# Moving more additions of a long convolution from VectorE to DMA, beside attention

## The chip, the cores and the metric

The kernel runs on one core of a Trainium2 chip. The metric is the time of one execution on the device in microseconds (us), the median of several runs. TensorE is called PE here, VectorE DVE, ScalarE ACT, GpSimd POOL and SyncE SP, as in the profile.

## The reference

Two independent halves are computed and set side by side. One is a state-space convolution over 576 channels: a kernel of 2048 taps is made for each channel from 128 complex modes, and applied as a causal convolution (the reference does it with a Fourier transform of twice the length). The other is attention with 32 query heads of width 18 that share one key and one value head. All is in float32.

```python
dt = exp(log_dt)[:, None];  A = A_re + 1j*A_im                      # [576, 128]
P = exp((dt*A)[:, :, None] * arange(2048))                           # [576, 128, 2048]
K = einsum("dn,dnl,dn->dl", C, P, dt*B).real                         # the taps
y = irfft(rfft(pad(u.T)) * rfft(pad(K)))[:, :2048].T + u * Dskip     # half A, [2048, 576]

q = (x @ wq) as 32 heads of 18;  k = x @ wk;  v = x @ wv             # x: [2048, 576]
p = softmax(q k^T * 18**-0.5);   o = p v                             # per head
out = concatenate([y, o @ wo], -1)                                   # [2048, 1152]
```

## The kernel before

**One planned order.** PE, ACT and DVE take their instructions in an order that the program itself writes out while it is built (`manual_schedule`); POOL and SP are ordered by the scheduler of the language. A small model of the clocks, `Clock` (`t` for PE, `v` for DVE, `a` for ACT), says when each engine would be free. The parts of the work are generators, wrapped in `Stream`. They yield what they need next: `"v"` with a time (go on once the clock is there), `"p"` (PE work, when there is room), `"w"` (ask again at the next step), `"b"` (a block of ACT work). On the chip nothing is timed by this model: it sets the order alone, and semaphores make each engine wait for its operands.

**Attention** (`Attention.main`) goes over 4 chunks of 512 queries, 8 groups of 4 heads, 16 blocks of 128 keys. For each of 1024 pairs of heads and key block, `scores` (L493) puts two matmuls into PSUM, `exponentials` (L504) is one ACT instruction of 128 x 1024, and `product` (L802) multiplies by the values. Three score buffers are in flight. Between the groups of three pairs, `fill` lets the other streams place work on PE: the projection of the next queries (`qproj`, `queries`), the output projection (`outproj`) and the convolution. Queries go to DRAM (`qd`, `sd`, on POOL's queue) and come back in another layout (`aug`, on SP's).

**The convolution** (`Conv`) goes over 12 chunks of 48 channels. Its `front(k)` makes the taps:

- `factors` (with `arguments`): exponentials, sines and cosines of 26 positions for each channel and mode; the modes lie on the partitions. For two chunks at a time ACT does them, and those of the odd chunk are put into DRAM (`park`) and loaded back. In `r` and `f` (real and imaginary part, `[P, 48, 26]`) the positions are innermost. `sm` is `r + f`, `df` is `f - r` for the last ten positions.
- `tables(k, s)`, twice a chunk (`NSB = 2`, 24 channels each): each power is the product of two factors. For each of three groups of columns DVE does three products and two additions (the five rows of `tab` and `tt`).
- `kgen` (L1168): small matmuls of one part of the table with the other, 48 a bank, evacuated by DVE into `ksb`. The taps go through DRAM (`kd`) into `kt` with the partitions rearranged.

`back(k)` convolves. `transform` turns `u` and the taps into spectra `us` and `ks` with matmuls and DVE additions, and the sums of real and imaginary parts that the three-product form needs are added by DMA (L1240 for `us`, L1253 for `ks`). The time axis is four blocks, so the product of the spectra is a convolution over blocks: for each half of the rows (`h`), four products `pt` of shrinking size are added to `acc` by DVE. Then one DMA adds within `acc` (L1275), DVE combines, and the inverse transform `iy` adds onto `u * Dskip`, which is stored to `outa`.

**Front and back** are joined by `turn`: the streams are `back(k)` and `front(k + 1)`, and the next two begin when both have ended.

```python
        if self.n < NCK and not any(st.live for st in self.streams):
            self.n += 1
            k = self.n
            self.streams = [Stream(self.back(k, self.kt), self.k)] if k < NCK else []
            if k + 1 < NCK:
                self.streams.append(Stream(self.front(k + 1), self.k))
```

L128 and L132 are helper lines of `Vector`, through which nearly all of DVE's additions, products and copies go, and L202 one for matmuls; there the tiles' names tell the groups apart.

Of the kernel before, what the change touches and what calls it, by code (L numbers as in the profile page):

```python
# [17 lines left out]
P = 128  # L18
# [22 lines left out]
RATE = 3.6754  # L41
PACE = 2.761
AHEAD = 0.3494
TOTAL = 577.1437
LAST = 608.4461
DEFER = 0.378
NAUG = 5
LEFT = 2.1255
CAP = 1.4306
DEBT = 0.6525  # L50
GROUP = 0.1637
HOLD = 0.1219
LEAD = 1.5045
MOST = 0.4717
LEAST = 0.4946
NEAR = 0.9404
SLOPE = 0.7408
SOON = 1.1606
URGENT = 11.0338
BACK = 2  # L60
HELD = 0
GAP = 0.2773
GAP_NEW = 0.3388
# [5 lines left out]
NSB = 2  # L69
# [3 lines left out]
MAGIC = 12582912.0  # L73
TWO_PI = 6.283185
# [130 lines left out]
class Attention:  # L205
# [36 lines left out]
    def setup(self, tp, conv):  # L242
# [19 lines left out]
        self.ident = cp.tile([P, P], F32, name="ident")  # L262
# [159 lines left out]
    def queries(self, c, m, qh, ql, aw):  # L422
# [41 lines left out]
        sh = self.p2.tile([8, CT], F32R, tag="sh", name=f"sh{c}_{m}", bufs=1)  # L464
        V.tensor_scalar(sh, un[0:8, 0:1].broadcast_to([8, CT]), -1.0, None, op0=ALU.mult)
# [5 lines left out]
        q.dma_start(sd[h0 + n0:h1, :], sh[:h1 - h0 - n0, :].bitcast(F32))  # L471
# [495 lines left out]
class Conv:  # L967
# [57 lines left out]
    def arguments(self, k, w, f, r, m):  # L1025
# [11 lines left out]
        shp = [P, ND, NF]  # L1037
        ch = lambda t: t.unsqueeze(2).broadcast_to(shp)
        row = lambda j: self.pos[:, j, :].unsqueeze(1).broadcast_to(shp)
# [21 lines left out]
    def factors(self, k):  # L1061
# [4 lines left out]
        shp = [P, ND, NF]  # L1066
        ch = lambda t, n: t.unsqueeze(2).broadcast_to([P, ND, n])
# [4 lines left out]
        if k % 2:  # L1072
            n = ND * NF
            for j, t in enumerate((f, r, m, w)):
                nc.sync.dma_start(t, self.parked[:, j * n:min((j + 1) * n, 3 * n + 3 * ND)].rearrange("p (c n) -> p c n", n=t.shape[2]))
            yield "v", K.t + 7.0, False
        else:
            two = p1.tile([P, 3 * ND * NF + 3 * ND], F32, tag="tab", name=f"two{k}")
            part = lambda j, n: two[:, j * ND * NF:j * ND * NF + n * ND].rearrange("p (c n) -> p c n", n=NF if n == NF else ND)
# [26 lines left out]
        c8 = lambda t: t[:, :, 0:8]  # L1106
        t1 = p1.tile([P, ND, 8], F32, tag="tmp", name=f"t1_{k}")
        t2 = p1.tile([P, ND, 8], F32, tag="dif", name=f"t2_{k}")
        tt(t2, c8(r), ch(w[:, 1, :], 8), op=mu)
        tt(t1, c8(f), ch(w[:, 1, :], 8), op=mu)  # L1110
        yield "v", 0.0, False
        tt(c8(r), c8(r), ch(w[:, 0, :], 8), op=mu)
        tt(c8(f), c8(f), ch(w[:, 0, :], 8), op=mu)
# [3 lines left out]
        sm = p1.tile(shp, F32, tag="sum", name=f"sum{k}")  # L1117
        df = p1.tile([P, ND, 10], F32, tag="dif", name=f"dif{k}")
        yield "v", 0.0, False
        tt(df, f[:, :, 16:], r[:, :, 16:], op=sb)  # L1120
        yield "v", 0.0, False
        tt(sm, r, f, op=ad)
# [3 lines left out]
    def tables(self, k, s):  # L1126

        nc, V, p1 = self.nc, self.V, self.pf
        tt = V.tensor_tensor
        n = ND // NSB  # L1130
        r, f, sm, df = (t[:, s * n:(s + 1) * n, :] for t in self.fac)
        tab = p1.tile([P, 2, n, 96], F32, tag="tab", name=f"tab{k}_{s}")
        for j, t in enumerate((r, f)):
            V.tensor_copy(tab[:, j, :, 0:8], t[:, :, 0:8])
            V.tensor_copy(tab[:, j, :, 32:40], t[:, :, 8:16])

        for lo, hi, dst, j0, j1 in ((0, 16, 8, 0, 3), (8, 19, 40, 0, 4), (8, 19, 40, 4, 7)):
            nj = j1 - j0
            shp = [P, n, nj, 8]
            L = lambda t: t[:, :, lo:lo + 8].unsqueeze(2).broadcast_to(shp)  # L1140
            H = lambda t, o=0: t[:, :, hi - o + j0:hi - o + j1].unsqueeze(3).broadcast_to(shp)
            re, im = (tab[:, j, :, dst + 8 * j0:dst + 8 * j1].rearrange("p c (j l) -> p c j l", l=8) for j in range(2))
            t = p1.tile(shp, F32, tag="tmp", name=f"tt{k}_{s}_{lo}_{j0}")
# [3 lines left out]
            yield "v", 0.0, False  # L1147
            tt(t, L(f), H(sm), op=ALU.mult)
            yield "v", 0.0, False
            tt(im, im, re, op=ALU.add)  # L1150
            yield "v", 0.0, False
            tt(re, re, t, op=ALU.subtract)
            if (lo, j0) != (8, 4):
                yield "v", 0.0, False
        self.tab = tab

    def kgen(self, k, s, ksb):
        nc, K = self.nc, self.k
        tab = K.v + 0.3
        for q in range(2):  # L1160
            yield "p", max(tab, K.fill), False
            ps = self.bank(TB // 2 * 64, f"kg{k}_{s}_{q}").rearrange("p (d c) -> p d c", c=64)
            ds = slice(q * TB // 2, (q + 1) * TB // 2)
            for d in range(TB // 2):
                for j in range(2):
                    for g in range(4):
                        t = self.tab[:, j, g * TB + ds.start + d, :]
                        nc.tensor.matmul(ps[32 * g:32 * g + 32, d, :], t[:, :32], t[:, 32:],  # L1168
                                         start=(j == 0), stop=(j == 1), tile_position=(0, 32 * g))
            K.pe(0.665)  # L1170
            self.evacuate()
            self.V.tensor_copy(ksb[:, :, s, :, ds], ps.rearrange("p d (h c) -> p h c d", h=4))
            self.evacuated()

    def front(self, k):

        nc = self.nc
        yield from self.factors(k)
        ksb = self.pf.tile([P, 4, NSB, 16, TB], F32, tag="ksb", name=f"ksb{k}")
        for s in range(NSB):  # L1180
            yield from self.tables(k, s)
            yield from self.kgen(k, s, ksb)
# [48 lines left out]
    def back(self, k, kt):  # L1231
# [7 lines left out]
        nc.sync.dma_start(us[:, 0:4, :], us[:, 4:8, :])  # L1239
        nc.gpsimd.dma_start(us[:, 0:4, :], us[:, 8:12, :], accum_op=ALU.add)  # L1240
        ks = p1.tile([P, 12, NE], F32, tag="ks", name=f"ks{k}")
        yield from self.transform(lambda r: kt[:, :, :, 4 * r:4 * r + 4, :].rearrange("p g s b d -> p (g s) (b d)"), ks[:, 4:12, :], f"k{k}", self.kt_ready)
        self.kt = None
        k2, kd, ka = ks[:, 0:4, :], ks[:, 4:8, :], ks[:, 8:12, :]
        v = lambda t, b0, b1: t.rearrange("p q (c n) -> p (q c) n", n=4 * TB)[:, :, b0 * TB:b1 * TB]
# [5 lines left out]
        tt(kd, ka, k2, op=ALU.subtract)  # L1251
        yield "v", 0.0, False
        nc.gpsimd.dma_start(ka, k2, accum_op=ALU.add)  # L1253
        done = K.v + 8.0
        blk = lambda t, b0, b1: t.rearrange("p q (c b d) -> p (q c) b d", b=4, d=TB)[:, :, b0:b1, :]
        acc = p1.tile([P, 12, NE], F32, tag="acc", name=f"acc{k}")
        n = 6 * NE // TB // 4
        for h in range(2):
            if h == 1:
                yield "v", done, False  # L1260
            for m in range(4):
                shp = [P, n, 4 - m, TB]
                at = lambda t, b0, b1: blk(t, b0, b1)[:, h * n:(h + 1) * n]
                kb = at(ks, m, m + 1).broadcast_to(shp)
                if m == 0:
                    tt(at(acc, 0, 4), at(us, 0, 4), kb, op=ALU.mult)
                    yield "v", 0.0, False
                else:
                    t = p1.tile(shp, F32, tag="sc", name=f"pt{k}_{m}_{h}")
                    tt(t, at(us, 0, 4 - m), kb, op=ALU.mult)  # L1270
                    yield "v", 0.0, False
                    tt(at(acc, m, 4), at(acc, m, 4), t, op=ALU.add)
                    yield "v", 0.0, False
# [213 lines left out]
```

## Time and profile before

| | |
|---|---|
| three runs | 1188.77, 1191.43, 1191.72 us (median 1191.43) |
| the profiled execution | 1191.61 us, of which the span of its instructions is 1189.8 us |
| mean granted PE clock | 0.991 of full speed |
| bytes moved by DMA | 132.22 MB, mean 111 GB/s |

How to read it: a row of a group gives line, engine, operation, output and input tiles, shapes and count, then the busy time in us and the mean of one in ns, then how long the engine was idle just before these instructions and what ended that. The chain is the work that ended last, followed back from the last instruction; its shares say by which engine the time passed. A row of the timeline gives start, duration, engine, line and operation, and in brackets the idle time before it with what ended it. `x` is a count.

### The profile page before, as it was taken

To read this page: it belongs to the slowest core of one execution; us is meant where nothing else is said; L and a number is where in the kernel's file an instruction comes from. 1 tells how busy PE (TensorE), PEld (TensorE's weight loads), DVE (VectorE), ACT (ScalarE), POOL (GpSimd) and SP (SyncE) were. 2 spreads that over 40 slices of the span, in tenths; PEclk is the share of its full clock that TensorE was granted. 3 is DMA by queue.
4 is the path that set the end of the run, shared out by engine and by line. 5 is a ranking of instruction groups with operands and counts; after the bars stand their busy time and mean duration, and the time that the engine had idled before them with its cause. 6 is when DMAs were issued, how large, how long until landed. Compare 5 with 4: busy or idle time off the path is not lost.

```text
span 1189.8 us, 41346 instructions
## 1 busy us (share of the span) xinstructions
PE 1136.8 (96%) x17954; PEld 604.1 (51%) x17954; DVE 960.9 (81%) x1698; ACT 1039.8 (87%) x1095; POOL 86.9 (7%) x140
## 2 busy tenths in 40 slices
PE   7999999998999989999989999999999999999997
PEld 2455555554555545555545555544544545555553
DVE  6858969885996996697799699699699797699485
ACT  5999889987888988988898888998999998899993
POOL 1100200101010100011020000001000000000000
PEclk9999999999999999999989999999999999999999
DMA  8542444425232331424353421234422431431222
GB/s 297 169 143 74 137 140 100 151 80 183 65 121 81 103 128 66 154 64 115 110 172 103 152 73 50 98 98 130 140 72 66 131 122 58 156 88 39 90 56 70
DMA packets 57097, 132.22 MB, mean 111 GB/s; under 512 B 7732, under 2 KB 18068, under 8 KB 55631
## 3 DMA queue, kind: packets, MB, share of 16 engines
q1 hardware_dynamic: 45647, 100.60, 24.4%
q0 software_dynamic: 10544, 28.19, 10.0%
q8 instruction: 143, 2.34, 0.8%
q10 hardware_dynamic: 720, 0.73, 0.2%
q14 instruction: 43, 0.35, 0.1%
HBM read 61.51 MB, written 48.45 MB: 92 GB/s over the span
## 4 chain that ended last, share of the span: by engine, by line
PE 64%; DVE 23%; ACT 5%; DMA 4%; issue 3%; SPq 0%; ACTq 0%; DVEq 0%
PE ops L802 26%; PE s L493 18%; DVE tab L128 6%; DVE acc L128 3%; PE op L202 3%; PE q L202 3%; ACT P L504 3%; PE iy L202 3%; PE kg L1168 3%; DVE ks L128 2%; DVE pt L128 2%; PE lk L202 1%; PE hk L202 1%; PE lu L202 1%; DVE tt L128 1%
## 5 line engine op out<-in xcount | busy, mean ns | idle before, releaser
L504 ACT ACTIVATE P<-s 128x1024 f32<-128x1024 f32 x992 | 941.6, 1031 | 114.3 <-PE s L493 105.6
L802 PE MATMUL ops<-P,v_sb 128*32 128x256 f32 x8192 | 536.1, 383 | 4.4 <-DVE o L132 2.8
L493 PE MATMUL s<-aug,kaug 55*128 55x512 f32 x2048 | 350.8, 439 | 7.1 <-ACT P L504 6.0
L802 PEld LDWEIGHTS ops<-P,v_sb 128*32 128x32 f32 x8192 | 247.2, 110 | 185.8 <-issue 52.2
L493 PEld LDWEIGHTS s<-aug,kaug 55*128 55x128 f32 x2048 | 167.9, 185 | 201.9 <-ACT P L504 107.9
L202 PE MATMUL op<-wo_sb,oT 126*32 126x288 f32 (+1 forms) x1152 | 84.3, 410 | 8.2 <-DVE ob L132 7.6
L202 PE MATMUL q<-x,wq_sb 128*32 128x256 f32 x1200 | 79.3, 390 | 4.5 <-DVE ql L128 2.4
L132 DVE COPY ksb<-kg 128x192 f32<-128x192 f32 x48 | 17.6, 367 | 66.3 <-PE kg L1168 66.1
L128 DVE TENSOR_TENSOR tab<-tab,tt 128x576 f32<-128x576 f32 (+1 forms) x72 | 59.1, 820 | 1.3
L128 DVE TENSOR_TENSOR tab<-sum,r 128x576 f32<-128x576 f32 (+1 forms) x72 | 58.7, 816 | 0.0
L128 DVE TENSOR_TENSOR tt<-f,sum 128x576 f32<-128x576 f32 (+1 forms) x72 | 58.7, 815 | 0.0
L128 DVE TENSOR_TENSOR tab<-tab 128x576 f32<-128x576 f32 (+1 forms) x72 | 58.7, 815 | 0.0
L128 DVE TENSOR_TENSOR tab<-r,dif 128x576 f32<-128x576 f32 (+1 forms) x72 | 58.7, 815 | 0.0
L128 DVE TENSOR_TENSOR acc<-acc,pt 128x864 f32<-128x864 f32 (+2 forms) x72 | 54.4, 755 | 1.7
L202 PEld LDWEIGHTS op<-wo_sb,oT 126*32 126x32 f32 (+1 forms) x1152 | 32.4, 109 | 45.1 <-DVE ob L132 13.1
L202 PEld LDWEIGHTS q<-x,wq_sb 128*32 128x32 f32 x1200 | 36.2, 111 | 36.7 <-issue 11.3
L128 DVE TENSOR_TENSOR pt<-us,ks 128x864 f32<-128x864 f32 (+2 forms) x72 | 54.0, 750 | 0.6
L1240 POOL DMA_DIRECT2D us<-us x12 | 11.8, 980 | 517.0 <-PE lk L202 84.6
L1168 PEld LDWEIGHTS kg<-tab 128*32 128x32 f32 x2304 | 36.7, 110 | 13.9 <-issue 5.9
L128 DVE TENSOR_TENSOR scu<-lu,scu 128x384 f32<-128x384 f32 x48 | 24.5, 551 | 23.6 <-PE lu L202 23.5
L1168 PE MATMUL kg<-tab 128*32 128x64 f32 x2304 | 41.8, 220 | 1.5 <-DVE tab L128 0.9
L128 DVE TENSOR_TENSOR u<-u,iy 128x384 f32<-128x384 f32 x24 | 13.3, 554 | 32.8 <-PE iy L202 32.8
(162 smaller groups left out, 1039.5 us busy)
## 6 DMA issues: line engine op xcount, KB each, us to landing
aug<-qd SPq DMA_DIRECT2D x124, 108.0 KB
park<-two SPq DMA_DIRECT2D x6, 1944.0 KB
od<-o SPq DMA_DIRECT2D x31, 256.0 KB
qd<-qh POOLq DMA_DIRECT2D x30, 256.0 KB, 3.5
u<-u SPq DMA_DIRECT2D x12, 480.0 KB
kd<-ksb SPq DMA_DIRECT2D x12, 384.0 KB
kt<-kd SPq DMA_DIRECT2D x48, 96.0 KB
us<-us SPq DMA_DIRECT2D x12, 384.0 KB
```

The lines of the kernel that those rows point to most:

```text
L128: return self.v.tensor_tensor(out, a, b, **k)
L132: return self.v.tensor_copy(out, src)
L202: nc.tensor.matmul(ps[j:e], w[:, j:e], x, start=start, stop=stop, tile_position=(0, j))
L493: nc.tensor.matmul(ps[:, j, :], self.kaug[r, kb * P:(kb + 1) * P], t[r, :], start=True, stop=True)
L504: nc.scalar.activation(pt, ps, AF.Exp, scale=SCALE)
L802: nc.tensor.matmul(o_ps[32 * j:32 * j + 32, cs], self.v[:, kb, :], pts[2 * n + j // 2][:, j % 2, cs], start=(kb + f == 0), stop=(kb + f == ...
L1168: nc.tensor.matmul(ps[32 * g:32 * g + 32, d, :], t[:, :32], t[:, 32:], start=(j == 0), stop=(j == 1), tile_position=(0, 32 * g))
L1240: nc.gpsimd.dma_start(us[:, 0:4, :], us[:, 8:12, :], accum_op=ALU.add)
```

## The change

- **Tables.** Four sub-blocks of 12 channels instead of two of 24. DVE does three products a group and no addition: two are written into the table, and the third, `t`, is added by one DMA on POOL's queue to real and imaginary part alike (`t` is read twice). Two table buffers alternate, and `kgen` of a sub-block comes after the products of the next. The groups have 3, 3 and 4 rows of eight columns. Three `t` buffers.
- **Order of dimensions.** In `r`, `f`, `sm`, `df` and the tables the channels are innermost. A column of the table that `kgen` hands to PE has its words 12 apart. In the spectra the blocks come before the channels.
- **Factor sums.** The middle eight positions of `sm` are made by a copy and an addition on POOL's queue; DVE makes the first eight and, for the last ten, `-(r) - f`.
- **Accumulators.** The three products of a half go into one tile; DVE adds the third to the second, and two DMAs on POOL's queue add them to `acc`.
- **Queues.** The copy into `us` moves from SP's queue to POOL's. POOL's instructions, too, are now in the program's order. The `sh` row of 512 words is written as 64 words that the store repeats; `ident` shares a buffer.
- **Streams.** `turn` goes: one stream runs all fronts, another all backs, and each waits only for `kt` (one buffer).
- **Constants.** The planner's pacing constants are other ones; a landing counts as `LAND = 7.0` us instead of 8.0.

```diff
-NSB = 2
+NSB = 4
+LAND = 7.0
...
-        sh = self.p2.tile([8, CT], F32R, tag="sh", name=f"sh{c}_{m}", bufs=1)
+        sh = self.p2.tile([8, 64], F32R, tag="sh", name=f"sh{c}_{m}", bufs=1)
...
+        nc.gpsimd.dma_start(sm[:, 8:16, :], r[:, 8:16, :])
+        nc.gpsimd.dma_start(sm[:, 8:16, :], f[:, 8:16, :], accum_op=ad)
+        self.sum_ready, self.free, self.landed = K.v + LAND + 3.0, [0.0] * 3, [0.0] * NSB
...
-        tt(sm, r, f, op=ad)
+        tt(c8(sm), c8(r), c8(f), op=ad)
+        V.scalar_tensor_tensor(sm[:, 16:, :], r[:, 16:, :], -1.0, f[:, 16:, :], op0=mu, op1=sb)
...
-        for lo, hi, dst, j0, j1 in ((0, 16, 8, 0, 3), (8, 19, 40, 0, 4), (8, 19, 40, 4, 7)):
...
-            tt(re, L(sm), H(r), op=ALU.mult)
-            tt(im, L(r), H(df, 16), op=ALU.mult)
-            tt(t, L(f), H(sm), op=ALU.mult)
-            tt(im, im, re, op=ALU.add)
-            tt(re, re, t, op=ALU.subtract)
+        for i, (lo, hi, dst, nj) in enumerate(((0, 16, 8, 3), (8, 19, 40, 3), (8, 22, 64, 4))):
...
+            tt(both[:, 1], L(r), H(df, 16), op=ALU.mult)
+            tt(both[:, 0], L(f), H(sm), op=ALU.mult)
+            yield "v", max(self.sum_ready if s == 0 and i else 0.0, self.free[i]), False
+            t = p1.tile(shp, F32, tag="tmp", name=f"p{k}_{s}_{i}", bufs=3)
+            tt(t, L(sm), H(r), op=ALU.mult)
+            nc.gpsimd.dma_start(tab[:, :, dst:dst + 8 * nj, :].rearrange("p i c n -> p i (c n)"),
+                                t.rearrange("p j l n -> p (j l n)").unsqueeze(1).broadcast_to([P, 2, nj * 8 * n]), accum_op=ALU.add)
+            self.free[i] = K.v + LAND
+        self.landed[s] = K.v + LAND
...
+        yield "p", max(self.landed[s], K.fill), False
+        ps = self.bank(TB * 64, f"kg{k}_{s}").rearrange("p (d c) -> p d c", c=64)
+                    t = tab[:, j, :, g * TB + d]
...
+        for s in range(NSB + 1):
+            if s < NSB:
+                if s > 1:
+                    yield "v", K.t + 0.3, False
+                yield from self.tables(k, s, tabs[:, s % 2])
+            if s > 0:
+                yield from self.kgen(k, s - 1, tabs[:, (s - 1) % 2], ksb)
...
-        nc.sync.dma_start(us[:, 0:4, :], us[:, 4:8, :])
+        nc.gpsimd.dma_start(us[:, 0:4, :], us[:, 4:8, :])
...
+            for m in (1, 2, 3):
+                tt(bl(t[m - 1]), bl(at(us, 0, 4 - m)), kb(m), op=ALU.mult)
+                if m == 1:
+                    nc.gpsimd.dma_start(at(acc, 1, 4), t[0], accum_op=ALU.add)
+            tt(v(t[1], 1, 2), v(t[1], 1, 2), t[2], op=ALU.add)
+            nc.gpsimd.dma_start(at(acc, 2, 4), t[1], accum_op=ALU.add)
+            done = K.v + LAND
+        yield "v", done, False
...
+    def fronts(self):
+        for k in range(NCK):
+            yield from self.front(k)
+            yield "v", 0.0, False
+
+    def backs(self):
+        for k in range(NCK):
+            while self.kt is None:
+                yield "w", 0.0, False
+            yield from self.back(k, self.kt)
...
-        with tc.manual_schedule(engines={mybir.EngineType.PE, mybir.EngineType.Activation, mybir.EngineType.DVE}):
+        with tc.manual_schedule(engines={mybir.EngineType.PE, mybir.EngineType.Activation, mybir.EngineType.DVE, mybir.EngineType.Pool}):
```

More of the change, by code (lines that the diff above doesn't have):

```diff
@@ L1331, in start @@
         self.load_u(1)
[L1333 to L1340 removed]
+        self.streams.append(Stream(self.backs(), self.k))
+    def fronts(self):
+        for k in range(NCK):
+            yield from self.front(k)
+            yield "v", 0.0, False
+    def backs(self):
[3 more added lines that the diff above has]
+            yield from self.back(k, self.kt)
     def go(self, step, credit, lock):
[L1343 removed]
         lag = step * RATE - self.work
@@ L1368, in drain @@
     def drain(self):
-        while self.streams:
+        while any(st.live for st in self.streams):
             for st in sorted(self.streams, key=lambda st: (not st.holds, st.work)):
```

194 lines of the change are left out of this document (80 added, 114 removed).

## The prediction

> **What bounds the kernel now.** I read the page first (busy shares, then the chain), then the busy time in stretches of 50 us.
>
> ```profile
> span 1189.8 us, 41346 instructions
> PE 1136.8 (96%) x17954; PEld 604.1 (51%) x17954; DVE 960.9 (81%) x1698; ACT 1039.8 (87%) x1095; POOL 86.9 (7%) x140
> PE 64%; DVE 23%; ACT 5%; DMA 4%; issue 3%; SPq 0%; ACTq 0%; DVEq 0%
> 0.00:50.00 50.00, 43.39 (x432) 18.68 (x432) 35.40 (x79) 34.36 (x38) 8.13 (x19) 0.93 0.74 262
> 250.00:300.00 50.00, 44.07 (x760) 23.82 (x754) 31.00 (x60) 37.98 (x41) 5.84 (x11) 0.94 0.40 134
> 600.00:650.00 50.00, 44.55 (x624) 22.36 (x620) 45.80 (x83) 44.34 (x47) 7.16 (x13) 0.93 0.47 155
> 850.00:900.00 50.00, 47.93 (x788) 25.44 (x776) 42.97 (x71) 46.71 (x50) 1.83 (x2) 1.00 0.32 94
> 1150.00:1200.00 50.00, 32.39 (x458) 15.85 (x458) 24.77 (x44) 19.22 (x22) 0.87 (x1) 0.97 0.15 48
> ```
>
> In the stretches the busy times stand in the order PE, weight loads, DVE, ACT, POOL, then the granted clock, the DMA share and GB/s. PE is the bound: it is idle for only 1189.8 - 1136.8 = 53.0 us. 6.6 us of that lie in the first stretch, and 39.8 - 32.4 = 7.4 us in the last 39.8 us. The other 39 us lie in the middle, most in stretches such as 250 to 300 (5.9 us) and 600 to 650 (5.4 us), where the clock also falls to 0.94 and 0.93. The chain puts 23% of the span, 274 us, on DVE: PE waits for it, a little at a time. One such place, from the timeline:
>
> ```profile
> 292.07 1.46 DVE L128 TENSOR_TENSOR r<-r,m 128x1248 f32<-128x1248 f32 x1 [6.11 <-DMA m<-park]
> 295.42 1.51 PE L202 MATMUL lu<-u,dft_sb 128*32 128x192 f32 x16 [5.32 <-DVE scu L132]
> ```
>
> Front 3 starts at the turn together with back 2. DVE stands 6.1 us behind its reloaded arguments, the evacuation `scu` is queued behind them, and PE, which takes its instructions in order, stops 5.3 us for `scu`. So DVE's lateness is what can be saved. No matmul is removed, and the 14 us of idle time at the two ends have other causes, so 39 us is about what this change can reach.
>
> **Part by part: what DVE loses.**
>
> ```profile
> L128 DVE TENSOR_TENSOR tab<-tab,tt 128x576 f32<-128x576 f32 (+1 forms) x72 | 59.1, 820 | 1.3
> L128 DVE TENSOR_TENSOR tab<-sum,r 128x576 f32<-128x576 f32 (+1 forms) x72 | 58.7, 816 | 0.0
> L128 DVE TENSOR_TENSOR tt<-f,sum 128x576 f32<-128x576 f32 (+1 forms) x72 | 58.7, 815 | 0.0
> L128 DVE TENSOR_TENSOR tab<-tab 128x576 f32<-128x576 f32 (+1 forms) x72 | 58.7, 815 | 0.0
> L128 DVE TENSOR_TENSOR tab<-r,dif 128x576 f32<-128x576 f32 (+1 forms) x72 | 58.7, 815 | 0.0
> L128 DVE TENSOR_TENSOR acc<-acc,pt 128x864 f32<-128x864 f32 (+2 forms) x72 | 54.4, 755 | 1.7
> L128 DVE TENSOR_TENSOR pt<-us,ks 128x288 f32<-128x288 f32 x24 | 10.7, 447 | 0.3
> L128 DVE TENSOR_TENSOR acc<-acc,pt 128x288 f32<-128x288 f32 x24 | 11.0, 457 | 0.7
> L128 DVE TENSOR_TENSOR t<-r,w 128x384 f32<-128x384 f32 x12 | 6.6, 548 | 0.0
> L128 DVE TENSOR_TENSOR dif<-f,r 128x480 f32<-128x480 f32 x12 | 7.8, 651 | 0.2
> L128 DVE TENSOR_TENSOR sum<-r,f 128x1248 f32<-128x1248 f32 x12 | 17.4, 1449 | 0.0
> L132 DVE COPY tab<-f 128x192 f32<-128x192 f32 x48 | 10.1, 252 | 0.0
> L128 DVE TENSOR_TENSOR w<-raw 128x48 f32<-128x48 f32 x24 | 4.8, 199 | 0.0
> L136 DVE TENSOR_SCALAR sh<-u 8x512 fp32r<-8x512 f32 x19 | 8.0, 419 | 0.7
> ```
>
> Tables: five operations a group now, 59.1 + 4 x 58.7 = 293.9 us. Afterwards each of 12 x 4 sub-blocks has three products for each of three groups, of 288, 288 and 384 words a partition. By the 288 and 384 rows, that is 48 x (6 x 0.447 + 3 x 0.548) = 207.7 us: 86 us less. The copies into the tables double in number and halve in size. The two kinds (`tab<-r` is like the `tab<-f` row) take 20 us now. 192 copies of 96 words cost between 20 us (half each) and 38 us (199 ns each, the 48-word row); I take 36, since the fixed part rules at this size: 16 us back. Tables together: 70 us less.
>
> Accumulators: of 54.4 us of additions, 24 of 288 words stay (11.0 us): 43 us less. Factor sums: 1449 ns a chunk become 548 + 651: 3 us less in twelve. The `sh` fill shrinks from 512 to 64 words a row, toward the 199 ns of the shortest row: 4 us less. DVE sheds 120 us in all and comes to some 841 us, 71%.
>
> The new orders of dimensions cost DVE nothing by my reading. The 288-word rows work on runs of 6 words, the 384 row on runs of 8; (548 - 447) / 96 is 1.05 ns a word, the slope that (1449 - 548) / 864 = 1.04 gives for whole rows. Runs of 12 and 48 lie between.
>
> What of the 120 us comes through? DVE stands on the chain for 274 of its 961 busy us, 28%. I give the removed work that share: 34 us. That is inside the 39 us that PE can give back; what is late next is PE itself, and ACT, with 50 exponentials in 50 us from 850 to 900, 46.7 us busy.
>
> The free streams remove no instruction. They let DVE do the one stream's work while the other waits, which I count as part of the same 34 us: in lockstep the added landings below would stand uncovered wherever the other stream has finished its part.
>
> **What is added: transfers, and waits on GpSimd's queue.**
>
> ```profile
> q0 software_dynamic: 10544, 28.19, 10.0%
> q1 hardware_dynamic: 45647, 100.60, 24.4%
> us<-us POOLq DMA_DIRECT2D x12, 384.0 KB, 4.4
> DMA to landing us min/median/max: 3.9/4.6/10.4
> L1275 POOL DMA_DIRECT2D acc<-acc x12 | 10.6, 886 | 147.1 <-DVE acc L128 145.4 <-DVE u L128 1.7
> POOL us L1240 <- DMA us<-us: 28.6, 1, 28.6
> 274.63 0.88 PE L1168 MATMUL kg<-tab 128*32 128x64 f32 x48
> L1168 PE MATMUL kg<-tab 128*32 128x64 f32 x2304 | 41.8, 220 | 1.5 <-DVE tab L128 0.9
> ```
>
> (The fourth row belongs to the tile `acc`.) Tables send 48 x 960 words x 2 x 512 B = 47 MB through GpSimd's queue, accumulators 12 x 2 x 1440 x 512 B = 18 MB, sums and the moved `us` copy 5 MB each: 75 MB on top of 28.2. By the q0 row that is about 26% of the DMA engines' time more, beside 34% for the two queues now; there is room. Issues: per chunk 12 for tables, 4 for accumulators, 2 for sums, 1 moved copy, so 228 at 0.89 us, 203 us of a queue that is 7% busy. The moved copy also frees SP of 12 issues and of its wait ahead of each.
>
> The wait is the dearer part. An accumulating transfer may only start when the write before it to the same bytes has landed; the row for L1240 shows GpSimd standing for such a copy. Afterwards it stands at four places a chunk: `us` copy then add, sum copy then add, and in each accumulator half the second add behind the first. Each lasts the 4.4 to 4.6 us of a landing, less about 1 us of work between. Queued behind are the table additions of the free-running front and the stores of the queries; for the tables, `kgen` on PE waits, and all of PE's queue behind it. On DVE the later table products wait for the sums, and the subtraction after both halves for the accumulators; behind these stand evacuations for PE, as with `scu` above. [...]
>
> The plan gives each landing 7.0 us, against a median of 4.6 and a longest of 10.4. A table landing that comes at the longest is 3.4 us late, and as PE stops in order I count it whole. With 48 table landings and 24 of sums and accumulators the bounds are nothing (none late) and 72 x 3.4 = 245 us (all). I take one in eighteen, 4 x 3.4 = 14 us, nearest the median row: a table block moves 288 to 384 KB, the size of those transfers.
>
> **PE's operands.** `kgen` now reads columns 12 words apart, where they were adjacent.
>
> ```profile
> L202 PE MATMUL hk<-kt,dft_sb 128*32 128x192 f32 x384 | 20.5, 331 | 0.3 <-DVE sck L128 0.3
> L202 PE MATMUL hu<-u,dft_sb 128*32 128x192 f32 x384 | 20.3, 329 | 0.8 <-DVE scu L128 0.8
> 280.97 0.86 PE L202 MATMUL hu<-u,dft_sb 128*32 128x192 f32 x16
> ```
>
> `hk` reads runs of 24 words with gaps, `hu` whole rows: 331 against 329 ns, so gaps alone cost nothing. No row has gaps after every word. Bounds: nothing (no matmul is saved, so not less), or `kg` twice as long. A group of 48 has a pitch of (0.88 - 0.22) / 47 = 14 ns by its rows, 0.67 us a group, 32 us in 48 groups: the upper bound is +32. The k transforms go to runs of three words: 16 matmuls at (0.86 - 0.33) / 15 = 35 ns, 48 such groups, at most +27. I take nothing for both, by the nearest row. [...]
>
> **Sum.** The profiled execution took 1191.6 us, 1.8 of them around the span; the median of three is 1191.4, so both serve. 1191.4 - 34 + 14 = 1171.4.
>
> **The rivals.**
> - *All the idle time in the middle goes.* The free streams take the turns away, as at 292 us, and no landing is late: 1191.4 - 39 = 1152. For it: DVE is only 31 of 50 us busy from 250 to 300, just where PE stops, so it is order rather than work that is missing there. Against: ACT needs its 1 us a pair. Chance 0.22.
> - *GpSimd's queue takes DVE's place* (slower). Sixteen of the 72 landings meet a standing GpSimd: 16 x 3.4 = 54, so 1191.4 - 34 + 54 = 1211. It decides from ten late ones (34 / 3.4). For it: GpSimd stands 48 x 3.5 = 168 us of about 1000. Against: 7.0 leaves 2.4 over the median. Chance 0.15.
> - *PE reads single words slowly* (slower). `kg` doubled: 1171.4 + 32 = 1203, and 1230 if the k transforms double too. It decides when `kg` takes 1.6 times as long (+20). Against: the `hk` row. Chance 0.15.
> - *DVE was not what PE waited for*; others come in its place at once: 1187 to 1195. For it: 96% on PE. Against: 23% of the chain. Chance 0.10.
>
> **How the numbers follow.** The forecast keeps 0.38, with 1158 to 1185 as its own range (none to eight late landings). Faster: 0.38 + 0.22 + 0.01 of the last rival = 0.61; within 0.3%, which is about what a measurement of this kernel can tell (3.6 us), 0.07; slower 0.15 + 0.15 + 0.02 = 0.32. The range from 1146 to 1213 holds the forecast, nearly all of the first rival, the last, and somewhat over half of the two slower ones.
>
> **What would show it.** Right: DVE near 841 us with no `tab<-tab` rows and 24 `acc` additions; matmul counts unchanged; `kg` at 0.22 us and 48 in about 0.88; POOL about 290 us busy; q0 near 103 MB; PE idle near 30 us; no longer waits at the turns. Wrong: PE waiting for `tab` transfers in `kg` for more than 30 us in all; 48 `kg` matmuls in over 1.3 us; landings with a median above 7 us; POOL rows waiting for DMA for hundreds of us.

## The result, and the profile after

| | median, us | lowest to highest | runs |
|---|---|---|---|
| before | 1191.58 | 1188.77 to 1192.17 | 4 |
| after | 1429.24 | 1420.96 to 1430.07 | 4 |

The change makes the kernel slower by a fifth: the ratio is 1.198, with a 95% interval from 1.194 to 1.203. The forecast was 1171.4 us; 1429 lies far above its range. The profiled execution took 1430.07 us.

From the page of the kernel after:

```profile
span 1428.3 us, 42011 instructions
PE 1225.4 (86%) x17954; PEld 654.8 (46%) x17954; DVE 830.9 (58%) x1830; ACT 1044.2 (73%) x1095; POOL 353.0 (25%) x368
q0 software_dynamic: 90800, 102.53, 44.0%
q1 hardware_dynamic: 43940, 95.88, 19.3%
L1166 PE MATMUL kg<-tab 128*32 128x64 f32 x2304 | 78.5, 298 | 61.7 <-DMA tab<-p 35.8
L203 PE MATMUL q<-x,wq_sb 128*32 128x256 f32 x1200 | 87.5, 416 | 26.4 <-DVE un L141 8.7
L1151 POOL DMA_DIRECT2D tab<-p x144 | 181.7, 1512 | 245.4 <-DVE p L129 95.1
```

DVE has lost 130 us of work, ten more than planned. But PE's idle time has gone from 53 to 1428.3 - 1225.4 = 203 us, and with the same 17,954 matmuls PE is busy 89 us longer. Of that `kg` has 37 us (41.8 before). The transforms of the taps, `hk` and `lk`, have 7 (20.5 each before, 24.2 and 24.1 now). The other 45 lie mostly in matmuls that the change doesn't touch, at a granted clock of 0.935 instead of 0.991: the projection `q` takes 416 ns, and before it took 390. The rows of `hk` after and of `q` before, by the groups with their forms apart:

```profile
L203 PE MATMUL hk<-kt,dft_sb 128*32 128x192 f32 x384 | 24.2, 367 | 3.9 <-DVE scu L129 2.7 <-DVE sck L129 1.2
L202 PE MATMUL q<-x,wq_sb 128*32 128x256 f32 x1200 | 79.3, 390 | 4.5 <-DVE ql L128 2.4 <-DVE un L140 1.6 <-DVE tab L128 0.4
```

The stretches quoted in the prediction, for the kernel after (columns: PE, weight loads, DVE, ACT, POOL, then granted clock, DMA share, GB/s):

```profile
250.00:300.00 50.00, 40.66 (x600) 21.95 (x595) 30.38 (x75) 35.17 (x38) 15.89 (x18) 0.90 0.70 162
600.00:650.00 50.00, 34.91 (x533) 19.47 (x535) 21.50 (x52) 26.12 (x28) 17.24 (x16) 0.83 0.79 140
850.00:900.00 50.00, 42.61 (x680) 24.60 (x676) 17.21 (x40) 35.48 (x40) 11.02 (x10) 0.93 0.64 122
```

PE, DVE and ACT are all idler than before, while the DMA engines' share has risen by two thirds to double: 0.40 to 0.70, 0.47 to 0.79 and 0.32 to 0.64. From 600 to 650 it does so at fewer GB/s (155 to 140). All three compute engines stand more than before, and the list of waits says for what. Each row has the total, the number and the longest in us:

```profile
ACT P L506 <- PE s L495: 311.2, 244, 16.3
DVE acc L129 <- DMA acc<-pt: 66.0, 11, 10.1
DVE pt L129 <- DMA acc<-pt: 56.3, 12, 9.3
DVE p L129 <- DMA tab<-p: 42.2, 28, 8.0
PE kg L1166 <- DMA tab<-p: 35.8, 10, 6.5
POOL sum L1112 <- DMA sum<-r: 43.7, 11, 7.1
POOL us L1243 <- DMA us<-us: 41.3, 11, 5.6
POOL acc L1279 <- DMA acc<-pt: 30.6, 6, 9.0
POOL acc L1275 <- DMA acc<-pt: 19.5, 3, 9.3
```

DVE alone stands 66.0 + 56.3 + 42.2 = 165 us for accumulating transfers to land (a landing is the time from a transfer's issue to the arrival of its data), and PE 35.8 us. Behind DVE's waits are evacuations for PE, and behind PE the scores that ACT waits for: 311 us here, where it was a third of that in the kernel before, by the same view:

```profile
ACT P L504 <- PE s L493: 105.6, 202, 7.8
```

How one half of the accumulators runs, from the timeline (start, duration, operation, and in brackets the idle time before it):

```profile
604.43 2.10 DVE L129 TENSOR_TENSOR pt<-us,ks 128x864 f32<-128x864 f32 x3 [9.11 <-DMA acc<-pt]
606.35 1.45 POOL L1272 DMA_DIRECT2D acc<-pt  x1 [1.78 <-DVE pt L129]
606.57 0.46 DVE L129 TENSOR_TENSOR pt<-pt 128x288 f32<-128x288 f32 x1
607.92 1.65 PE L1166 MATMUL kg<-tab 128*32 128x64 f32 x48 [7.30 <-issue]
611.30 2.85 ACT L506 ACTIVATE P<-s 128x1024 f32<-128x1024 f32 x3 [8.76 <-PE s L495]
613.90 1.42 POOL L1275 DMA_DIRECT2D acc<-pt  x1 [6.10 <-DVE tab L129]
614.74 3.00 POOL L1151 DMA_DIRECT2D tab<-p  x2
620.43 0.96 DVE L129 TENSOR_TENSOR acc<-acc 128x768 f32<-128x768 f32 x1 [6.83 <-DMA acc<-pt]
```

The first addition is issued at 606.35. The second goes onto the same words and is issued at 613.90, 7.6 us later, though DVE had its operand ready at 607.0 (606.57 + 0.46). (The row puts the end of that wait down to a table product of DVE, on which this addition doesn't depend; that it is the first addition's landing is tested below, in E15.) DVE's combination starts at 620.43: 13.4 us after DVE's last addition, where the plan had put 7.0. The table additions of the other stream queue up behind on POOL (614.74). The 9.11 us ahead of `pt` at 604.43 are the same wait for the half before, whose products lie in the buffers that are to be written.

### The profile page after: what moved, and what is told of

Same layout as the page of the kernel before. It is cut to its first block, busy times and chain, and to the rows that moved or that the text cites. A ratio compares the mean times of both kernels' runs of the same rounds, so it can differ in the third digit from the quotient of the medians.

```text
span 1428.3 us, 42011 instructions
## 1 busy us (share of the span) xinstructions
PE 1225.4 (86%) x17954; PEld 654.8 (46%) x17954; DVE 830.9 (58%) x1830; ACT 1044.2 (73%) x1095; POOL 353.0 (25%) x368
## 5 line engine op out<-in xcount | busy, mean ns | idle before, releaser
L804 PE MATMUL ops<-P,v_sb 128*32 128x256 f32 x8192 | 557.4, 392 | 3.8 <-DVE o L133 3.5
L1151 POOL DMA_DIRECT2D tab<-p x144 | 181.7, 1512 | 245.4 <-DVE p L129 95.1
L1166 PE MATMUL kg<-tab 128*32 128x64 f32 x2304 | 78.5, 298 | 61.7 <-DMA tab<-p 35.8
L1166 PEld LDWEIGHTS kg<-tab 128*32 128x32 f32 x2304 | 68.3, 147 | 77.5 <-issue 63.4
L129 DVE TENSOR_TENSOR p<-sum,r 128x288 f32<-128x288 f32 x144 | 69.9, 485 | 42.5 <-DMA tab<-p 42.2
L129 DVE TENSOR_TENSOR pt<-us,ks 128x864 f32<-128x864 f32 (+2 forms) x72 | 50.8, 751 | 56.3 <-DMA acc<-pt 56.3
L1275 POOL DMA_DIRECT2D acc<-pt x24 | 34.3, 1430 | 145.2 <-DVE tab L129 24.9
L129 DVE TENSOR_TENSOR tab<-f,sum 128x288 f32<-128x288 f32 x144 | 69.7, 484 | 0.0
L129 DVE TENSOR_TENSOR tab<-r,dif 128x288 f32<-128x288 f32 x144 | 69.7, 484 | 0.0
L203 PE MATMUL iy<-w,dft_sb 128*32 128x192 f32 x768 | 44.8, 368 | 25.5 <-DVE ksb L133 10.2
L1272 POOL DMA_DIRECT2D acc<-pt x24 | 34.7, 1448 | 62.1 <-DVE pt L129 62.1
L129 DVE TENSOR_TENSOR acc<-acc 128x768 f32<-128x768 f32 x12 | 11.4, 953 | 66.0 <-DMA acc<-pt 66.0
```

The source lines that it names most:

```text
L129: return self.v.tensor_tensor(out, a, b, **k)
L203: nc.tensor.matmul(ps[j:e], w[:, j:e], x, start=start, stop=stop, tile_position=(0, j))
L804: nc.tensor.matmul(o_ps[32 * j:32 * j + 32, cs], self.v[:, kb, :], pts[2 * n + j // 2][:, j % 2, cs], start=(kb + f == 0), stop=(kb + f == ...
L1151: nc.gpsimd.dma_start(tab[:, :, dst:dst + 8 * nj, :].rearrange("p i c n -> p i (c n)"), t.rearrange("p j l n -> p (j l n)").unsqueeze(1).b ...
L1272: nc.gpsimd.dma_start(at(acc, 1, 4), t[0], accum_op=ALU.add)
L1275: nc.gpsimd.dma_start(at(acc, 2, 4), t[1], accum_op=ALU.add)
```

## The experiments

Ratios stand to runs of the kernel before on the same chip (medians of 1191.7 to 1193.1 us), with their 95% intervals. "Constants refitted" means that the planner's pacing constants were chosen anew for that kernel, so that the plan's own clocks end earliest.

### Each part undone alone

**E1, `kgen` reads adjacent words.**

```diff
-                    t = tab[:, j, :, g * TB + d]
+                    t = tab[:, j].rearrange("p c n -> p (c n)")[:, 96 * (g * TB + d):96 * (g * TB + d) + 96]
```

> The changed kernel, but each small matmul of kgen reads 96 adjacent words of the same table buffer instead of 96 words that lie 12 apart (the taps are then not the right ones; instructions, waits and sizes are the same). Theory, late landings: kg falls from 1.65 to 0.88 us a group of 48, which gives back 48 x 0.77 = 37 us and not much more: 1380 to 1400 us. Rival, PE's strided operands are the main cause (they also make everything behind them late): below 1300 us. Rival, the new order of the streams: as the theory.

Measured: 1418.43 us, ratio 1.189 [1.181, 1.196], 11 us below the change, above the theory's range and far from the rival's. From the tile `tab`, the time of one matmul (min/median/max):

```profile
L1166 PE MATMUL kg<-tab x2304: 216/219/316, 60.2 to 1328.5; 128*32 128x64 f32 x192
```

The median falls from 297 to 219 ns, so the words 12 apart are what makes it slow. But of the 26 us by which `kg` is less busy (52.7 against 78.5) only 11 arrive: PE is idle 6 us longer (208.5 against 202.9), and its other matmuls take some 10 us longer, at a granted clock of 0.919 instead of 0.935. So the operands aren't the main cause here; their own price is left to E11.

**E2, the table additions on DVE. E3, the accumulators' additions on DVE. E4, both, and the factor sums as well.** The pacing constants stay; the order shifts, because the planner's clock counts the work added to DVE.

```diff
# E2, E4: tables
-            nc.gpsimd.dma_start(tab[:, :, dst:dst + 8 * nj, :]..., t..., accum_op=ALU.add)
+            for j in range(2):
+                tt(both[:, j], both[:, j], t, op=ALU.add)
# E3, E4: accumulators; for each m
-                    nc.gpsimd.dma_start(at(acc, 1, 4), t[0], accum_op=ALU.add)
+                tt(at(acc, m, 4), at(acc, m, 4), t[m - 1], op=ALU.add)
# E4: sums
-        nc.gpsimd.dma_start(sm[:, 8:16, :], f[:, 8:16, :], accum_op=ad)
+        tt(sm[:, 0:16, :], r[:, 0:16, :], f[:, 0:16, :], op=ad)
```

> The changed kernel with the 144 table transfers taken back: DVE adds the third product to both parts itself, 12 x 4 x (4 x 0.45 + 2 x 0.55) = 139 us of DVE more. Theory, late landings: the 42 us that DVE and the 36 us that PE wait for table transfers go, the queue of the DMA engines shrinks by 37 thousand packets, and the time falls by about half of the loss, to 1290 to 1350 us, although DVE works 139 us more. Rival, the order of the streams and the planner's constants: 1400 us or more. Rival, strided operands of kgen: 1400 or more.

> The changed kernel with the 48 accumulator transfers taken back: DVE adds all three products of each half to acc. DVE works about 43 us more. Theory, late landings: the 66 + 56 us that DVE stands for acc and pt go, less 43 us of work: 1330 to 1380 us. Rival, order of the streams: 1420 or more. Rival, strided operands: 1420 or more.

> The changed kernel with table, accumulator and sum transfers all taken back to DVE; the orders of dimensions, four sub-blocks, the free streams, GpSimd's program order and the constants stay. Theory, late landings: all of the loss but the 37 us of kgen's strided operands and some 7 us of the k transforms goes: 1225 to 1260 us. Rival, order of the streams and constants: above 1330 us. Rival, strided operands as the main cause: above 1330 us.

Measured: E2 1477.76 us, ratio 1.238 [1.231, 1.245]; E3 1377.17, 1.154 [1.147, 1.161]; E4 1368.80, 1.147 [1.138, 1.157]. E3 came in at the top of its range. E2 and E4 lie over 100 us above theirs, where their rivals had them. Why shows in the stretches at the end of E4:

```profile
1150.00:1200.00 50.00, 38.54 (x540) 19.11 (x532) 38.92 (x65) 42.31 (x44) 1.72 (x2) 0.93 0.29 91
1200.00:1250.00 50.00, 14.52 (x276) 8.90 (x280) 43.49 (x112) 0.00 (x0) 0.57 (x1) 0.50 0.16 56
```

Attention is done at 1187; after that ACT is at 0 and the convolution goes on alone for another 167 us, on DVE, with PE at half its clock. The constants meter out the convolution for a DVE that has less to do. E2 and E3 end the same way: from the last exponential to the last store of the convolution 136 and 107 us pass, where the kernel after has 9. So undoing an edit in this kernel tests edit and plan together, none of the three times says what the transfers cost, and that E3 lies within its range is luck. E5 and E8 were made for that.

### The transfers cut short, and the plan fitted

**E8, everything in the change's order, but each accumulating transfer of tables and accumulators cut to a piece.** Issues, waits and instructions stay.

```diff
-            nc.gpsimd.dma_start(tab[:, :, dst:dst + 8 * nj, :]..., t..., accum_op=ALU.add)
+            nc.gpsimd.dma_start(tab[:, 0, dst:dst + 8, :], t[:, 0], accum_op=ALU.add)
-                    nc.gpsimd.dma_start(at(acc, 1, 4), t[0], accum_op=ALU.add)
+                    nc.gpsimd.dma_start(at(acc, 1, 4)[:, 0], t[0][:, 0], accum_op=ALU.add)
```

> The changed kernel, instruction for instruction in the same order and with the same constants and waits; only the table transfers add one block of 96 words to one part instead of 288 or 384 words to two, and the accumulator transfers one row of six (the rest of those additions is left out, so the taps and the convolution are not the right ones). Theory, late landings against an order that counts on 7.0 us: landings fall under 5 us, PE's and DVE's waits for tab, pt and acc nearly go, and of the loss only the strided kgen stays: 1210 to 1260 us. Rival, the order itself (free streams, constants): above 1350 us. Rival, GpSimd's own issue time and program order, whatever the size: above 1300 us.

Measured: 1241.19 us, ratio 1.040 [1.036, 1.044]: 188 us of the change's 238 hang on the size of these transfers. Its waits:

```profile
DVE pt L129 <- DMA acc<-pt: 7.5, 3, 5.0
DVE p L129 <- DMA tab<-p: 6.4, 3, 5.7
PE kg L1166 <- DMA tab<-p: 1.9, 2, 1.5
```

The same waits stand there, at 7.5 for 56.3, 6.4 for 42.2 and 1.9 for 35.8 us; `acc` behind `acc<-pt` is gone from the list. A table addition lands in a median of 3.7 us instead of 7.6, an addition of `pt` to `acc` in 2.5 to 2.8 instead of 4.8 to 6.2. The landings of the tables, in the kernel after and in E8:

```profile
DMA to landing us min/median/max: 4.1/7.6/13.8
DMA to landing us min/median/max: 2.2/3.7/9.1
```

**E5, E4 with constants refitted** and a group of `kgen` costed at 1.39 us instead of 0.665, as the timeline has it.

```diff
-            K.pe(0.665)
+            K.pe(1.39)
```

> e4_all_dve with the planner's constants refitted: kgen costed at 1.39 us as the trace has it, and the pacing constants chosen so that, by the plan's own clock, the convolution ends close to the end of attention instead of 137 us behind it. Theory: the 167 us in which e4 works off the convolution alone mostly go: 1225 to 1260 us, that is the kernel before plus 37 us for kgen and some 7 us for the k transforms. Rival, the new order of streams is slow by itself: above 1300 us.

Measured: 1242.42 us, ratio 1.041 [1.038, 1.045], as expected. What E4 had above this, 126 us, was the misfitted plan. E5 and E8 agree to 1 us: with no such transfers, or with small ones, the change's new layouts and streams run at 1241 to 1242 us. As E5 has other constants and 164 us more work on DVE (989.7 against 826.2), the closeness of the two may be in part chance.

**E6, the change with constants refitted** for a landing of 12 us.

```diff
-LAND = 7.0
+LAND = 12.0
```

> The changed kernel with all its transfers, but planned with LAND = 12.0 us and kgen at 1.39 us, and the pacing constants refitted to that. Theory, the order counted on landings that come later: waits of DVE and PE for transfers fall to a third and the time to 1270 to 1310 us. Rival, the transfers load the DMA engines so much that any order stalls: above 1370 us. Rival, strided kgen as the main cause: above 1370 us.

Measured: 1429.69 us, ratio 1.198 [1.191, 1.205]: nothing gained. The time is where the two rivals had it (above 1370 us), but the trace doesn't show that the load stalls any order, because this plan has a fault of its own, described below. DVE still stands for the accumulators about as long as in the kernel after:

```profile
DVE acc L129 <- DMA acc<-pt: 64.2, 11, 10.7
```

Waits on other tiles did shrink (`pt` from 56.3 to 23.5 us, `p` from 42.2 to 23.8), but the exponentials ended at 1294 and 108 us of convolution followed, as in E3 and E4: this plan puts the convolution off. So E6 decides between neither of its theories.

### The parts that are no transfers

**E7, the kernel before with the free streams alone; E10, the kernel before with nothing but constants refitted.** E10 is E7's control.

```diff
# E7 alone; turn goes as well
-        self.streams = [Stream(self.front(0), self.k)]
+        self.streams = [Stream(self.fronts(), self.k)]
...
+        self.streams.append(Stream(self.backs(), self.k))
```

> The kernel before with one part of the change alone, the free streams (turn goes, one stream of fronts and one of backs), and pacing constants refitted by the plan's own clock. Theory, the free streams are harmless: 1185 to 1210 us. Rival, the free streams are what costs: above 1280 us. The forecast's first rival, that they end the stalls at the turns: below 1180 us.

> The kernel before, only its pacing constants refitted by the plan's own clock, starting from those of the changed kernel; no part of the change. A control for the refitted runs: it shows how far equal plans differ on the chip. Theory (constants matter little when the plan is as good): 1180 to 1205 us, and then the 28 us of the free streams alone are theirs. Rival, refitted constants are worse by themselves: 1210 to 1230 us, as with the free streams alone.

Measured: E7 1220.61 us, ratio 1.023 [1.020, 1.027]; E10 1198.77, 1.004 [1.002, 1.007]. E10 is within its range; E7 lies between its theory (up to 1210) and its rival (above 1280). So refitting costs 6 us at these constants, and the free streams a further 22, by one refit of each. The forecast had counted them as part of the gain; PE's idle time in E7 is 67 us instead of 53.

**E11, E8 with E1's adjacent words**: both edits above.

> e8_short (transfers cut short, so most of those additions left out) with kgen reading adjacent words as in e1. Where PE does not wait for landings, the strided operands show their own price: 48 x 0.77 = 37 us less than e8_short, 1200 to 1210 us. Rival, PE has slack there and the price is hidden: 1225 us or more.

Measured: 1208.14 us, ratio 1.014 [1.005, 1.022], as expected. Beside E8 that makes 33 us for the strided operand of `kgen`, where PE hardly waits for landings. From the page:

```profile
PE 1144.8 (95%) x17954; PEld 605.5 (50%) x17954; DVE 826.1 (68%) x1830; ACT 1044.3 (87%) x1095; POOL 278.1 (23%) x368
```

This is what the change would be with quick landings and adjacent words: DVE 135 us less busy than before, PE 8 us more (most of it `hk` and `lk` at 367 ns), and the time 16 us above the kernel before (5 to 27 by the interval). Net of all that came with it, DVE's relief bought nothing.

### The transfers taken apart

**E9, one addition for each half of the accumulators** (DVE folds the other products; constants refitted).

```diff
-                if m == 1:
-                    nc.gpsimd.dma_start(at(acc, 1, 4), t[0], accum_op=ALU.add)
+                if m > 1:
+                    tt(v(t[0], m - 1, 3), v(t[0], m - 1, 3), t[m - 1], op=ALU.add)
-            nc.gpsimd.dma_start(at(acc, 2, 4), t[1], accum_op=ALU.add)
+            nc.gpsimd.dma_start(at(acc, 1, 4), t[0], accum_op=ALU.add)
```

> The changed kernel, but with one accumulator transfer a half instead of two: DVE folds the second and third product into the first (864 words more a half, less the 288 of now: 24 x 0.75 = 18 us of DVE more), then one transfer adds the three blocks to acc. Pacing constants refitted by the plan's own clock. No second add stands behind a first. Theory, the chained pair of landings (two of 6 to 7 us where the plan counts one of 7.0) is the larger part of the loss: the 66 + 56 us that DVE waits for acc and pt fall to about 30, and the time to 1310 to 1350 us. Rival, the load of the transfers on the DMA engines, whatever their order: 1390 us or more. Rival, tables: 1400 or more.

**E12, tables and sums by DMA, the accumulators' additions on DVE**, `LAND` 10.0, `kgen` at 1.39, constants refitted: E3's edit with a plan made for it.

> e3_acc_dve (tables and sums by DMA, accumulators by DVE) planned with LAND = 10.0 us and kgen at 1.39 us, pacing constants refitted. Theory: a table landing stands alone, with a median of 7.6 us and no chain, so a plan with room for it hides most: 1250 to 1285 us, against 1242 for e5 with all additions on DVE. Rival, table transfers cost by their load whatever the plan: above 1310 us.

Measured: E9 1354.73 us, ratio 1.137 [1.126, 1.147]; E12 1292.90, 1.085 [1.074, 1.095]; both just above their ranges. With the second landing gone, DVE's two waits for the accumulators come to 22.6 + 15.4 = 38 us, from 122. E12 is 50 us above E5, so even a plan that allows 10 us for each landing of the tables doesn't hide them. But not all of the 50 is theirs: after the last exponential E12 works 35 us to the last store of the convolution, E5 only 9, and that end of the plan is about half of the difference.

**E13, only the tables' transfers cut short; E14, only the accumulators'; E15, the second addition of each half goes into `us`**, whose words no other addition awaits. In E15 sizes and issues stay; nothing is refitted in the three.

```diff
-            nc.gpsimd.dma_start(at(acc, 2, 4), t[1], accum_op=ALU.add)
+            nc.gpsimd.dma_start(at(us, 2, 4), t[1], accum_op=ALU.add)
```

> The changed kernel, same order and constants, only the table transfers cut to 96 words (most of those additions left out). If the tables' landings are the larger part: below 1320 us. If the accumulators' pair is the larger part: 1340 to 1390 us; a share of the accumulators' waits goes too, since their landings share the DMA engines.

> The changed kernel, same order and constants, only the accumulator transfers cut to one row of six (most of those additions left out); the second add still stands behind the first. If the accumulators' pair is the larger part: 1290 to 1340 us. If the tables are: 1370 us or more.

> The changed kernel, same order, constants and sizes; the second accumulator add of each half goes into the same rows of us, which are no longer needed, instead of acc (so acc lacks those products). GpSimd need not wait for the first landing. If the chain of two landings is what costs: as e14, 1300 to 1350 us. If the load of the transfers is: 1390 us or more.

Measured: E13 1355.28 us, ratio 1.136 [1.130, 1.142]; E14 1312.13, 1.100 [1.094, 1.106]; E15 1350.63, 1.132 [1.126, 1.138]. Each is from one pair of runs that differ by 1.5 us at most. The waits of E13, E14 and E15, in this order:

```profile
DVE pt L129 <- DMA acc<-pt: 60.2, 12, 8.9
DVE acc L129 <- DMA acc<-pt: 50.4, 11, 8.0
DVE p L129 <- DMA tab<-p: 6.9, 3, 6.1
```

```profile
DVE pt L129 <- DMA acc<-pt: 6.9, 3, 4.9
DVE p L129 <- DMA tab<-p: 47.3, 27, 8.5
PE kg L1166 <- DMA tab<-p: 24.7, 8, 7.1
```

```profile
DVE p L129 <- DMA tab<-p: 45.4, 26, 8.3
DVE pt L129 <- DMA us<-pt: 23.5, 9, 5.5
```

Short tables take 74 us off and leave the accumulators' waits; short accumulators take 117 off and leave the tables'; 191 together, where E8, with both short, takes 188. So the two hardly overlap. E15 takes 79 of the 117 with every byte still moved, and E9, which has one landing a half by another edit, comes within 4 us of it, with a refitted plan. E15's timeline shows what is gone:

```profile
584.72 1.45 POOL L1272 DMA_DIRECT2D acc<-pt  x1 [6.93 <-DVE pt L129]
584.93 0.46 DVE L129 TENSOR_TENSOR pt<-pt 128x288 f32<-128x288 f32 x1
585.68 1.93 POOL L1275 DMA_DIRECT2D us<-pt  x1
591.89 0.95 DVE L129 TENSOR_TENSOR acc<-acc 128x768 f32<-128x768 f32 x1
```

The second addition follows the first by 1.0 us instead of 7.6, and DVE combines 6.5 us after its last addition (585.39, that is 584.93 + 0.46) instead of 13.4, without standing still. So GpSimd's wait was for the first landing. E15 also frees DVE's combination from the second landing, which now goes to words that it doesn't read; the 79 us are the price of both, of a second landing behind the first and of a reader behind the second. That is two thirds of the accumulators' cost; a third is the size and the load. E15 came in just outside the range of the chain's theory (1300 to 1350) and far from that of the load's (1390 and above).

## Where the 238 us are, and which steps failed

The runs make a ledger (medians, each from the difference of two kernels). Below its first step all kernels have one order and the same constants:

| step | us | from |
|---|---|---|
| before | 1191.6 | |
| streams, constants, POOL's order, runs of three words, less work on DVE, the short transfers | +16 | E11 - before |
| `kgen`'s words 12 apart | +33 | E8 - E11 |
| tables' transfers, beyond 96 words | +74 | after - E13 |
| accumulators' second landing | +79 | after - E15 |
| accumulators' size and load | +38 | E15 - E14 |
| sum | 1432 | measured 1429.2 |

- **What bounds the kernel.** That PE was the bound stands; the step from there to a gain failed. *DVE's share of the chain times the removed work* (34 us) isn't what removed work is worth. In E11 135 us of DVE work are gone, the streams are free, the landings are short, and net nothing comes back. This isn't the last rival, *DVE was not what PE waited for*: PE's waits for DVE add up to 33.6 us in the kernel before and to 41.6 in E11. It still waits for DVE, which has less to do and comes as late. The longest of these rows in the kernel before and in E11:

```profile
PE op L202 <- DVE ob L132: 7.6, 8, 2.8
PE up L203 <- DVE aw L137: 9.1, 7, 3.3
```

How much of E11's 16 us is the relief, the streams and the runs of three words was not separated. In E7, where DVE has its full work, the streams go with 48.3 us of such waits (41.2 in E10) and a time 12 us above E11's, so some of the relief may have come through.

- **DVE's own sum** was right within 10 us: 831 us for the 841 forecast. The mean of `p` is 485 ns for the three sizes together, against (2 x 447 + 548) / 3 = 481 in the working, and a copy of 96 words took 203 ns for 36 / 192 = 188.
- **Free streams.** Taken as part of the gain, because DVE could work for one stream while the other waits. E7 beside E10 makes it a loss of 22 us. What in the order costs it the runs don't show.
- **Landings, the step that failed most.** *One in eighteen late, 14 us*: measured 191, against the same transfers cut short. Three things in that step were wrong. First, the count of landings: *"LAND = 7.0"* was set against a single landing, though the working itself said that the second addition of a half waits for the first. Two landings in series are what DVE's combination waits for, 13.4 us in the timeline against 7.0. And the 24 landings of "sums and accumulators" have one a chunk for the accumulators, where DVE waited for them 11 + 12 = 23 times in 24 halves. (The row for L1240 is a single wait of 28.6 us, so it shows that GpSimd waits, but not what one landing costs.) Second, the size of a landing: 4.6 us came from a queue with 28 MB; a table block took 7.6 in the median and 13.8 at the longest. Part of that is load: the addition within `acc`, unchanged in size, landed in 4.6 us before and in 8.3 after, and in 4.7 where the transfers of tables and accumulators are short (E8), though other additions of its size still took 4.5:

```profile
acc<-acc POOLq DMA_DIRECT2D x12, 384.0 KB, 4.6
acc<-acc POOLq DMA_DIRECT2D x12, 384.0 KB, 8.3
us<-us POOLq DMA_DIRECT2D x24, 384.0 KB, 4.5
```

The first row is of the kernel before. Third, the load was priced by bytes: 26% of the DMA engines more, where q0 went from 10.0% of 1189.8 us to 44.0% of 1428.3. That is 509 us of all sixteen engines for 74 MB, 0.15 MB a us against 0.24 before. E2, without the tables' transfers, and E3, without the accumulators', give the rate of each part by what is missing from q0 (of 1476.0 and 1374.1 us, in this order):

```profile
q0 software_dynamic: 51632, 55.33, 21.1%
q0 software_dynamic: 53168, 84.83, 34.0%
```

The tables' 47.2 MB went at 0.15 MB a us in packets of 1.2 KB, the accumulators' 17.7 MB at 0.11 in packets of 0.47 KB, and the queue of the kernel before has 2.67 KB a packet. In these three the rate falls with the packet, from 0.24 by 0.15 to 0.11; that the packets alone make it no run shows. The upper bound, 245, held. The rival with GpSimd's queue was right in kind, and its waits in size (135 us of the 168 it named). But DVE stands at least as long, and 54 us was too small by the same count of late landings.

- **PE's operands.** *I take nothing for both, by the nearest row*: the nearest row was the wrong one. Runs of 24 words cost nothing (331 against 329 ns); single words cost `kgen` 33 us (E8 - E11). The +32 and +27 that stood as bounds, and the third rival with them, took the matmuls at twice their time; that factor was an estimate, and no run then on hand showed it. Measured: a group of 48 matmuls went from 0.88 to 1.65 us, 1.9 times, with one matmul at 297 ns on words 12 apart and at 219 on adjacent ones. The k transforms, at runs of three words, went from 331 to 367 ns, 7 us of PE in all, in E11 too, where the granted clock is 0.989.
- **The signs named in advance.** PE waiting in `kgen` for tables over 30 us (35.8), 48 `kg` in over 1.3 us (1.65) and landings over 7 us (the tables' 7.6) all came. POOL's waits for DMA came to 135 us in the rows above, short of the hundreds named.

No version beat the kernel before; the best, E10, is that kernel with other constants, at 1198.8 us.

## What to carry to other kernels

Here the work moved from DVE to accumulating transfers was paid in landings, 74 + 79 + 38 = 191 us of the ledger. So count how many stand in series on the same words before the reader may go, price each by a transfer of its own kind under the load that the change itself makes, not by its bytes at the rate of another queue, and ask which engine stops in order behind the wait. DVE's share of the chain didn't say what its removed work was worth: in E11 it has 135 us less to do, and PE waits for it 41.6 us where it waited 33.6. A run that makes the cost of the replacement small, as E11 does, tells what the change could have gained. In a kernel with a written-out order an edit undone alone also undoes the fit of the order, so fit it again, look whether one part of the work runs on alone at the end, and keep a control that is refitted and otherwise unchanged.

## What the runs showed of the hardware

- Small matmuls (128 x 32 weights, 64 columns) with operand words 12 apart took 297 ns instead of 219, their weight loads 144 instead of 110, and a row of 48 had a pitch of 29 ns, (1.65 - 0.30) / 47, instead of 14. In E1 and E11 the same matmuls on adjacent words were back at 219.
- In the kernel after, accumulating transfers of 288 to 432 KB landed in medians of 4.2 to 8.9 us, by group: 4.2 for `ks`, 4.8 and 6.2 for `pt` onto `acc`, 7.2 and 8.9 for the tables, 8.3 within `acc`. Cut to 96 words or one row (48 to 72 KB), they took 2.5 to 3.7 in E8. On GpSimd the issues of table additions kept the queue busy for 1.26 us each (181.7 / 144), where the additions within `acc` took 0.89 before.
- In four stretches PE's granted clock was the lower the idler PE was: 1.00 where it was busy 47.9 of 50 us (kernel before, 850 to 900), 0.93 at 42.6 and 0.83 at 34.9 (kernel after, 850 to 900 and 600 to 650), 0.50 at 14.5 (E4, 1200 to 1250). Not all stretches fall in line: E4 has 0.93 at 38.5 from 1150 to 1200. Matmuls that the change doesn't touch were longer in the kernel after: `q` took 416 ns at a mean clock of 0.935, and 388 in E8, with the same matmuls, at 0.989. From this I take it that the 45 us of longer matmuls in the kernel after come with the waits; no run separates the two.
